# A listed order of operations, seven chunk maxima instead of eight, and the 1e-9 moved off VectorE, in a fused top-32 attention and tanh-softplus MLP kernel

## The chip, the cores and the metric

The kernel runs on one core of one Trainium2 chip. The metric is device time in microseconds (us): the median of three runs before the change is 825.11 us (824.66 to 825.91). The work is spread over TensorE (PE), VectorE (DVE), ScalarE (ACT), GpSimd (POOL) and the DMA queue that SyncE (SP) feeds.

## The reference

What is computed, for 4 batches of 8 heads, 576 positions and a head dimension of 64, then 2304 tokens of width 512 through a hidden width of 2048:

```python
scores = scale * np.matmul(q, k.transpose(0, 1, 3, 2))
kth = np.partition(scores, -32, axis=-1)[..., -32:-31]
scores = np.where(scores >= kth, scores, -1e9)
scores = scores - np.max(scores, axis=-1, keepdims=True)
attn = np.exp(scores)
attn = attn / (np.sum(attn, axis=-1, keepdims=True) + 1e-09)
x = np.matmul(attn, v)                      # then heads side by side: 2304 x 512
h = x @ w_in                                # 512 -> 2048
sp = np.where(h > 20.0, h, np.log1p(np.exp(np.minimum(h, 20.0))))
out = (h * np.tanh(sp)) @ w_out             # 2048 -> 512
```

## The kernel before

**Attention.** Work comes in 80 units; a unit is one pair of heads and 128 query rows of each (two row tiles, 64 units) or the last 64 rows of both heads (one row tile, 16 units): 144 row tiles in all. For each row tile, PE multiplies queries by keys in two halves of 288 columns (L593), and ACT copies each half out of PSUM into the tile S (L612). DVE takes the eight largest values of each of eight chunks of 72 columns with MAX8 (L627), and from these 64 candidates three times the eight largest (L637, with a match-and-replace between, L641): the 24th largest candidate. It counts how many scores lie below that (L660 on DVE, or L656 on ACT), POOL clears the larger ones (L664), and one MAX8 over the whole row (L670) gives the true 32nd largest, whatever up to eight large values the candidates had missed. ACT takes the exponent (L734), DVE masks it and sums it (L736), DVE adds 1e-9 to the sum (L742, one instruction per row tile) and takes the reciprocal (L743). In the first 21 units the reciprocal is spread (L751) and multiplied in at the very end; in the units after them (`divided`) the row itself is multiplied by it (L764 on POOL or L766 on ACT). PE transposes the weights (L789), ACT copies them (L795); the last pieces are transposed apart (L804 to L808, called the tail here), ACT copies these (L813, tile WX), and PE multiplies with the values (L827, called AV here). The result goes to `xr` (L841 to L848 on DVE, L868 on ACT).

**MLP.** Nine groups of 256 tokens. Each is split into a high and a low part (L923 to L934), so that fp32 products come from three fast matmuls: layer 1 is 144 sets of 12 matmuls (L957) and layer 2 is 144 sets of six (L1042; four plain ones, L1038, in the first group). ACT makes the activation between them (L963 to L989), POOL multiplies and splits (L1004 to L1019). While the first groups run, the weights are unpacked and split; that of some weight tiles goes through PE (L507, L508).

**Order.** `Plan.schedule()` orders the program before it is built: each operation has a cost, its dependencies, a priority and sometimes several engines (`also`); the planner takes the operation that can begin first, by its costs, and the order in which they come out is the order of each engine's queue. The numbers at the head of the file (`OFF`, `LAG`, `CB`, `LB`, ...) are its priorities and choices. PE, DVE, ACT and POOL each run their queue in order, so an instruction that waits holds everything behind it. Where PE would idle in the plan, throw-away matmuls (`filler`, L1162) are put in. A second program follows for inputs in which a row's candidates missed more than eight values; it is branched over (`missed`).

Of the kernel before, what the change touches and what calls it, by code (L numbers as in the profile page):

```python
# [2 lines left out]

# [10 lines left out]
AF = mybir.ActivationFunctionType  # L14
ALU = mybir.AluOpType
# [7 lines left out]

THREE = 2.0 ** -29 * (1 - 2.0 ** -14)
HALF = 0.5 - 2.0 ** -12
NCH = 8
PAD = 9

DIVIDED = 21
HUGE = 1.0e38  # L30
GT = 256
NU = 2
# [6 lines left out]
MLP0 = 76.30575001803295  # L39
MLPS = 1.2378480913699303  # L40
LAG = (-40.12243341145539, -38.28909365751999, -32.8778952976761, -78.28015271904145, -52.599446352806034, -50.1764095795117, -49.69230946190221, -93.44342581700634, 42.99260706506286)
OFF = (-170.39780068367187, -64.02958231418937, -74.2557654138884, 7.857637984216179, -16.336484036288216, -27.809736477494315, -70.41929461728364, -109.81289668550335, -354.7823787851044, -3.8461291151298846, -8.182769269493052, 3.2344209413047413, 6.677364896275946)
WPO = 10.505571910776663
CB = (0, 1, 2, 3, 4, 5, 6, 7, 9, 12, 13, 14, 15, 16, 17, 18, 19, 20, 21, 22, 23, 24, 25, 27, 30, 32, 33, 34, 35, 36, 39, 41, 42, 43, 44, 46, 47, 49, 53, 55, 65, 78, 103, 105, 108, 120, 128, 137)
MB = (0, 4, 5, 10, 14, 16, 21, 31, 34, 35, 42, 45, 74, 134, 135, 143)
PBO = (0, 2, 6, 8, 10, 12)
PBH = (0, 6, 9, 10, 16, 20, 28, 31)
WPR = (13.170210396787844, 0.40696336778296444)
DELTA = {'pe': 0.1566540244821026, 'dve': 0.05973313251400048, 'act': 0.16389989721877987, 'pool': 0.0006081253308147598, 'sp': 0.0}
LOADW = 0.6048073411328094  # L50
ALSO = True
PLAIN = ()
LOST = (0, 1, 2, 3, 4, 5, 6, 8, 9, 10, 12, 13, 14)
LATER = 1
NST = 3
X = (-40.29362652876879, -6.877857684025652)
LOCK = True
BEHIND = 6.0
GATE = 0.17
TAB = 1.295  # L60
BIAS = [(61.900462734716776, 1.2804919633935512), (566.4514881009378, 0.8850565354570911), (1000000000.0, 0.3893476774127522)]
LB = (0, 1, 3, 5, 6, 7, 8, 10, 12, 13, 14, 16, 19, 20, 25, 30)
SB = (6, 10, 15, 17, 25, 30)
PH = {}

SLACK = {'pe': 0.0, 'dve': 0.005961469571805072, 'act': 0.07441473974429097, 'pool': 0.048459337826946364}

CHAIN = 46.48753167278615  # L70
# [33 lines left out]
class Plan:  # L104
# [29 lines left out]
    def schedule(self):  # L134
        free = {p: [(0.0, i) for i in range(n)] for p, n in self.sizes.items()}
# [14 lines left out]
        ndone = 0  # L150
# [3 lines left out]
        loaded, window, left = "exp", None, 0  # L154
# [14 lines left out]

        while ndone < len(self.ops):  # L170
            best = {}
            for c in cand:
                o, rs = c
                if o.tab and window and (o.tab == "exp" or o.tab[1] != window):
                    continue
                pr = pool_ready(o) if o.alloc else 0.0
                if pr is None:
                    continue
                w = None
                for x, (e, d, _) in enumerate(o.ways):  # L180
# [23 lines left out]
            o = c[0]  # L204
# [97 lines left out]
def attn_moe_kernel(  # L302
# [17 lines left out]
    T = S // 128  # L320
    L = S - T * 128
    HS = S // 2
    CW = S // NCH
    NG = NT // GT
    scale = 1.0 / math.sqrt(D)
    Z = SIZES
# [73 lines left out]
    def build(fast, weights):  # L400
# [157 lines left out]
        def unit(b, p, t, pkey, kready, vready, last, pr, final):  # L558
# [59 lines left out]
            if fast:  # L618
# [1 line left out]
                Ct = lambda n: g_("C", ck[n])  # L620
                cur = [None] * nt
                for n in range(nt):
                    per = NCH // 2
                    for e in range(2):
                        def mx(n=n, e=e):
                            for j in range(e * per, (e + 1) * per):
                                nc.vector.max(Ct(n)[:, j, :], St(n)[:, j * CW:(j + 1) * CW])  # L627
                        al = [("C", ck[n])] if e == 0 else []
                        if n == 0 and e == 0:
                            al += [("M8", m8k), ("SM", smk)]  # L630
                        dd = [sready[n][e], cur[n]]
# [598 lines left out]
```

## Time and profile before

| | |
|---|---|
| median of three runs | 825.11 us |
| profiled execution, its own time | 824.54 us |
| its span, first to last instruction | 822.7 us |
| PE busy | 773.6 us (94%) |
| DVE busy | 685.1 us (83%) |
| ACT busy | 631.4 us (77%) |
| POOL busy | 561.0 us (68%) |
| mean granted PE clock | 0.981 of full speed |

Busy is the time in which at least one instruction of an engine was under way; DVE and PE overlap the end of one instruction with the start of the next, so the pace of a row of equal instructions is read from their starts, not from the duration of one. A wait in the profile names the instruction that came late and the one that released it.

### The profile page before, as it was taken

What the parts mean: (1) busy time and instruction counts of PE and PEld (TensorE: products, weight loads), DVE (VectorE), ACT (ScalarE), POOL (GpSimd) and SP (SyncE); (2) the same over time, 40 slices, a digit from 0 to 9 for tenths busy, and PEclk for the clock granted to TensorE, in tenths of its full rate; (3) what the DMA queues carried; (4) which work ended last, traced back from release to release, by engine and by line L of the source; (5) the groups of instructions that cost most, each with busy time, mean ns of one, the idle gap of its engine ahead of it and who ended that gap; (6) DMA issues with size and microseconds to landing.
All of it is one profiled execution on the core that took longest, in us unless ns stands there. A gap on an engine that the chain in (4) does not pass through costs nothing.

```text
span 822.7 us, 18268 instructions
## 1 busy us (share of the span) xinstructions
PE 773.6 (94%) x5698; PEld 604.1 (73%) x5698; DVE 685.1 (83%) x3344; ACT 631.4 (77%) x1245; POOL 561.0 (68%) x821
## 2 busy tenths in 40 slices
PE   7988999988998899999989999999999999999996
PEld 5556578656667687878857777778878787788884
DVE  7999999998898899998999899899999998715031
ACT  6889899898897687978797567887887698556380
POOL 4888786889898887697688775688666565703111
PEclk9999999996999999999999999999999999999998
DMA  4444346782224233231123332222322213403322
GB/s 155 131 127 125 99 145 202 228 284 89 89 95 144 61 93 93 67 110 38 40 64 95 109 101 85 65 82 79 91 82 73 80 59 91 128 21 92 102 75 83
DMA packets 56795, 83.73 MB, mean 102 GB/s; under 512 B 5872, under 2 KB 28656, under 8 KB 56688
## 3 DMA queue, kind: packets, MB, share of 16 engines
q1 hardware_dynamic: 56464, 82.19, 32.7%
q8 instruction: 47, 0.77, 0.4%
q14 instruction: 60, 0.49, 0.2%
q10 hardware_dynamic: 224, 0.28, 0.1%
HBM read 66.72 MB, written 8.13 MB: 91 GB/s over the span
## 4 chain that ended last, share of the span: by engine, by line
PE 65%; DVE 14%; POOL 9%; ACT 7%; issue 3%; DMA 1%; SPq 0%; DVEq 0%; POOLq 0%
PE psH L957 20%; PE psO L1042 18%; PE psW L593 8%; PE psW L827 7%; PE psW L789 6%; POOL Y L664 3%; DVE Y L736 3%; DVE C L627 3%; PE psO L1038 2%; PE psW L957 2%; DVE M L670 2%; DVE Y L660 2%; DVE M L637 1%; DVE C L641 1%; ACT mb L963 1%
## 5 line engine op out<-in xcount | busy, mean ns | idle before, releaser
L664 POOL TENSOR_TENSOR Y<-Y,S 128x576 f32<-128x576 f32 x126 | 177.4, 1419 | 37.7 <-DVE Y L736 13.3
L627 DVE MAX8 C<-S 128x8 f32<-128x72 f32 x1152 | 176.3, 219 | 13.6 <-ACT S L612 13.5
L957 PE MATMUL psH<-xh,wih 128*128 128x256 f32 x528 | 158.8, 301 | 6.3 <-ACT mb L963 5.5
L957 PE MATMUL psH<-xl,wih 128*128 128x256 f32 x528 | 148.1, 280 | 0.6 <-POOL xl L928 0.6
L957 PE MATMUL psH<-xh,wil 128*128 128x256 f32 x528 | 147.8, 280 | 0.0
L1019 POOL TENSOR_TENSOR GL<-mb,GH 128x256 fp32r<-128x256 f32 x102 | 74.7, 736 | 78.0 <-PE psO L1042 61.2
L593 PE MATMUL psW<-KS,QS 64*128 64x288 f32 (+1 forms) x576 | 117.7, 457 | 5.5 <-ACT S L612 2.9
L612 ACT COPY S<-psW 128x288 f32<-128x288 f32 x288 | 100.7, 407 | 22.9 <-PE psW L593 21.5
L670 DVE MAX8 M<-Y 128x8 f32<-128x585 f32 x144 | 109.5, 762 | 9.7 <-POOL Y L664 7.9
L957 PEld LDWEIGHTS psH<-xh,wih 128*128 128x128 f32 x528 | 99.8, 189 | 20.4 <-ACT mb L963 8.5
L734 ACT ACTIVATE Y<-S,SM 128x576 f32<-128x576 f32 x121 | 92.8, 783 | 25.1 <-DVE M L670 24.6
L736 DVE SCALAR_TENSOR_TENSOR Y<-S,M,Y 128x576 f32<-128x576 f32 x121 | 103.2, 876 | 8.2 <-ACT Y L734 7.9
L1042 PE MATMUL psO<-woh,GH 128*128 128x512 f32 x256 | 108.3, 423 | 0.0
L957 PEld LDWEIGHTS psH<-xl,wih 128*128 128x128 f32 x528 | 100.0, 189 | 1.3 <-POOL xl L928 0.8
L957 PEld LDWEIGHTS psH<-xh,wil 128*128 128x128 f32 x528 | 99.8, 189 | 0.0
L789 PE MATMUL psW<-ident,Y 128*128 128x128 f32 (+1 forms) x640 | 85.3, 276 | 12.8 <-POOL Y L764 4.3
L795 ACT COPY WT<-psW 128x512 f32<-128x512 f32 (+1 forms) x159 | 80.9, 547 | 20.1 <-PE psW L789 19.4
L789 PEld LDWEIGHTS psW<-ident,Y 128*128 128x128 f32 (+1 forms) x640 | 66.6, 144 | 37.9 <-POOL Y L764 8.9
L827 PE MATMUL psW<-WT,V 128*64 128x128 f32 (+1 forms) x1280 | 82.3, 272 | 10.6 <-ACT WX L813 10.6
L827 PEld LDWEIGHTS psW<-WT,V 128*64 128x64 f32 x1280 | 64.4, 139 | 32.5 <-ACT WX L813 16.2
L593 PEld LDWEIGHTS psW<-KS,QS 64*128 64x128 f32 (+1 forms) x576 | 58.7, 192 | 37.0 <-issue 12.3
L660 DVE TENSOR_SCALAR_CACHE_REDUCE Y<-S,M 128x576 f32<-128x576 f32 x96 | 77.0, 806 | 7.9 <-PE psW L806 6.1
(155 smaller groups left out, 1748.2 us busy)
## 6 DMA issues: line engine op xcount, KB each, us to landing
WL<-wld SPq DMA_DIRECT2D x104, 256.0 KB, 2.7
V<-in_v_dram SPq DMA_DIRECT2D x28, 320.0 KB, 3.0
mb<-in_moe_w_in_dram SPq DMA_DIRECT2D x16, 512.0 KB, 3.9
mb<-in_moe_w_out_dram SPq DMA_DIRECT2D x16, 512.0 KB, 4.2
KS<-in_k_dram SPq DMA_DIRECT2D x27, 288.0 KB, 2.9
QS<-in_q_dram SPq DMA_DIRECT2D x80, 64.0 KB, 2.1
woh<-mb SPq DMA_DIRECT2D x16, 256.0 KB, 3.3
wld<-woh SPq DMA_DIRECT2D x13, 256.0 KB, 2.4
```

The lines of the kernel that those rows point to most:

```text
L593: nc.tensor.matmul(psW[P.slot[wks[n]]][:, 0:HS], g_("QS", qs)[hp, :], KSt()[hp, rng], start=True, stop=True)
L612: return lambda: eng(St(n)[:, rng], psW[P.slot[w]][:, 0:HS])
L627: nc.vector.max(Ct(n)[:, j, :], St(n)[:, j * CW:(j + 1) * CW])
L660: c = P.op("dve", dve(S, 60), lambda n=n, c24=c24, lt=lt: nc.vector.tensor_scalar(Yt(n), St(n), c24(), None, op0=ALU.is_lt, op1=ALU.add, a ...
L664: y = either(pool2(S), held(S), lambda eng, n=n: eng.tensor_tensor(Yt(n), Yt(n), St(n), op=ALU.mult), [c], prio=pr + 0.5 + OFF[5])
L670: ym.append(P.op("dve", dve(S + PAD), lambda n=n: nc.vector.max(M8()[:, n, 3, :], Yw(n)), [y, x], prio=pr + 0.6 + OFF[6]))
L734: e = P.op("act", acts(S, 1), lambda n=n: nc.scalar.activation(Yt(n), St(n), AF.Exp, scale=scale, bias=SM()[:, 0, n:n + 1]), [nm, ym[n]], ...
L736: mk.append(P.op("dve", held(S, 68), lambda n=n: nc.vector.scalar_tensor_tensor(Yt(n), St(n), th(n), Yt(n), op0=ALU.is_ge, op1=ALU.mult, a ...
L789: nc.tensor.transpose(psW[P.slot[wk]][:, t_ * w:(t_ + 1) * w], Yt(n)[hp, c_:c_ + 128], ident[hp, hp])
L827: nc.tensor.matmul(psX[64 * h:64 * h + 64, 0:n_], lw, rhs, start=t_ == 0, stop=t_ == T)
L957: nc.tensor.matmul(w, a, b_, start=n == 0, stop=n == len(mm) - 1)
L1042: nc.tensor.matmul(psO[t], c[:, ts_], y, start=f == 0 and n == 0, stop=f == NF - 1 and n == 2)
```

## The change

Four things. (1) `CHUNKS` replaces the eight chunks of 72 columns by seven of 83 or 82; three of them lie in the first half of S, four end in the second. The tiles of candidates have 56 values, not 64. (2) The two instructions per unit that add 1e-9 leave DVE; one instruction on POOL or ACT adds it for the whole unit, and the reciprocal on DVE waits for that. (3) `DIVIDED` goes from 21 to 20, and the planner's numbers are others. (4) The first program's order is no longer what the planner picks: `listed()` unpacks a string of numbers, one operation and one choice of engine each, and `schedule()` takes the operations in that order (it still works out when each would start, and the queues follow these starts).

```diff
-NCH = 8
+CHUNKS = (83, 83, 82, 82, 82, 82, 82)
-DIVIDED = 21
+DIVIDED = 20
-LB = (0, 1, 3, 5, 6, 7, 8, 10, 12, 13, 14, 16, 19, 20, 25, 30)
+LB = (0, 1, 3, 5, 7, 8, 10, 13, 14, 20, 22, 24, 27, 29, 31)
...
+ORDER = (
+    b"c-m!G2OyR2_rLCS-97ES_uiF^>^&pNXoyG}8cIb)*`rCzC|X7(gp8<2Q8Fq*i!_KdQ1XAC_r2)*`=5L7^PKZJpYu8AdEQGIc>DU@kR_29W6gZ?"
...
+def listed():
+    x = np.frombuffer(zlib.decompress(base64.b85decode(ORDER)), np.uint8).reshape(2, -1).astype(int)
+    x = x[0] + 256 * x[1]
+    return [(int(n) & 8191, int(n) >> 13) for n in x]
...
         while ndone < len(self.ops):
             best = {}
+            want, only = self.listed[ndone] if self.listed else (None, None)
             for c in cand:
                 o, rs = c
-                if o.tab and window and (o.tab == "exp" or o.tab[1] != window):
+                if self.listed:
+                    if o.seq != want:
+                        continue
+                elif o.tab and window and (o.tab == "exp" or o.tab[1] != window):
                     continue
...
                 for x, (e, d, _) in enumerate(o.ways):
+                    if only is not None and x != only:
+                        continue
...
-                        def mx(n=n, e=e):
-                            for j in range(e * per, (e + 1) * per):
-                                nc.vector.max(Ct(n)[:, j, :], St(n)[:, j * CW:(j + 1) * CW])
+                        js = [j for j in range(NCH) if (EDGE[j + 1] > HS) == e]
+
+                        def mx(n=n, js=js):
+                            for j in js:
+                                nc.vector.max(Ct(n)[:, j, :], St(n)[:, EDGE[j]:EDGE[j + 1]])
...
             def rz():
-                for n in range(nt):
-                    nc.vector.tensor_scalar(SM()[:, 3, n:n + 1], SM()[:, 2, n:n + 1], 1e-9, None, op0=ALU.add)
                 nc.vector.reciprocal(SM()[:, 4, 0:nt], SM()[:, 3, 0:nt])

-            rzo = P.op("dve", 0.25, rz, mk + [lg], free=[("M8", m8k)], prio=pr + 0.8 + OFF[6])
+            rzo = P.op("pool", 0.15, lambda: nc.gpsimd.tensor_scalar(
+                SM()[:, 3, 0:nt], SM()[:, 2, 0:nt], 1e-9, 0.0, op0=ALU.add, op1=ALU.add), mk, prio=pr + 0.8 + OFF[6],
+                also=[("act", acts(nt), lambda: nc.scalar.activation(
+                    SM()[:, 3, 0:nt], SM()[:, 2, 0:nt], AF.Copy, bias=1e-9))] if ALSO else ())
+            rzo = P.op("dve", 0.13, rz, [rzo, lg], free=[("M8", m8k)], prio=pr + 0.8 + OFF[6])
```

Two places show what that does to the queues. The first is DVE's queue at the reciprocal of the 26th unit (SM is the tile of that unit's sums, Y its weights, C the candidates, M8 the maxima). Before:

```order
L736 SCALAR_TENSOR_TENSOR Y_1_92,SM_1_106<-S_4_89,M8_1_103,Y_1_92 128x576
L736 SCALAR_TENSOR_TENSOR Y_1_92,SM_1_106<-S_5_90,M8_1_103,Y_1_92 128x576
L627 MAX C_1_117<-S_3_88 128x8 x4
L742 TENSOR_SCALAR SM_1_106<-SM_1_106 128x1 x2
L743 RECIPROCAL SM_1_106<-SM_1_106 128x2
L797 COPY WT_1_100<-psW3_127 128x512
```

The same unit in the changed kernel:

```order
L845 SCALAR_TENSOR_TENSOR Y_1_92,SM_1_106<-S_4_89,M8_1_103,Y_1_92 128x576
L875 TENSOR_SCALAR Y_0_91<-Y_0_91,SM_0_105 128x576
L845 SCALAR_TENSOR_TENSOR Y_1_92,SM_1_106<-S_5_90,M8_1_103,Y_1_92 128x576
L736 MAX C_0_116<-S_3_88 128x8 x7
L850 RECIPROCAL SM_1_106<-SM_1_106 128x2
L746 MAX M8_0_102<-C_0_116 128x8
```

The two additions are gone from this queue, seven chunk maxima stand between the last sum and the reciprocal, and one multiplication of an earlier unit's row (L875) has come over from POOL.

The second is PE's queue at the tail and the AV of the 59th unit (psW is the PSUM bank of the attention, WT and V its weights and values, psO that of layer 2). Before:

```order
L593 MATMUL psW_124<-KS_93,QS_97 128x288
L593 MATMUL psW_126<-KS_93,QS_97 128x288
L806 MATMUL psW_125<-ident,Y_91 128x128
L827 MATMUL psW_125<-WT_99,V_98 64x128
L827 MATMUL psW_125<-WT_100,V_98 64x128
```

The same unit in the changed kernel:

```order
L917 MATMUL psW_125<-ident,Y_91 128x128
L1153 MATMUL psO<-woh,GH_110 128x512
L1153 MATMUL psO<-WL_82,GH_110 128x512
L1153 MATMUL psO<-woh,GL_113 128x512
L1153 MATMUL psO<-woh,GH_110 128x512
L1153 MATMUL psO<-WL_82,GH_110 128x512
L1153 MATMUL psO<-woh,GL_113 128x512
L701 MATMUL psW_127<-KS_93,QS_97 128x288
L701 MATMUL psW_126<-KS_93,QS_97 128x288
L938 MATMUL psW_125<-WT_99,V_98 64x128
L938 MATMUL psW_125<-WT_100,V_98 64x128
```

Between the tail (L806, now L917) and the AV (L827, now L938) of one unit there stood nothing; now a set of layer 2 and a pair of scores stand there.

## Rows read from the trace of the kernel before

**Rows 1.** Busy time by stage, with the granted PE clock (1.00 is full)

```profile
core 0: us, PE busy (x) PEld busy (x) DVE busy (x) ACT busy (x) POOL busy (x), PEclk, DMA share, GB/s
0.00:107.20 107.20, 93.33 (x597) 61.65 (x597) 97.34 (x522) 88.96 (x203) 80.05 (x144) 0.98 0.42 126
107.20:538.20 431.00, 408.47 (x3137) 315.45 (x3133) 396.69 (x1997) 348.80 (x696) 339.29 (x469) 0.97 0.35 109
538.20:721.80 183.60, 181.25 (x1383) 146.90 (x1382) 167.36 (x778) 145.07 (x277) 124.69 (x184) 1.00 0.28 85
721.80:815.20 93.40, 90.47 (x589) 80.06 (x588) 23.71 (x51) 47.63 (x68) 17.01 (x26) 1.00 0.26 76
815.20:822.70 7.50, 0.04 (x1) 0.00 (x0) 0.00 (x0) 0.92 (x3) 0.00 (x0) 0.69 0.28 76
```

**Rows 2.** What PE waited for: total us, times, longest

```profile
PE psW L827 <- ACT WX L813: 10.6, 16, 1.6
PE psH L957 <- ACT mb L963: 5.5, 11, 1.0
```

**Rows 3.** Busy time from 184 to 200 us, columns as in rows 1

```profile
184.00:200.00 16.00, 13.86 (x84) 10.54 (x83) 14.52 (x73) 13.83 (x27) 14.15 (x22) 0.50 0.30 107
```

**Rows 4.** DVE in order of time: start, us, line, operation, count

```profile
480.40 0.20 DVE L742 TENSOR_SCALAR SM<-SM 128x1 f32<-128x1 f32 x2
480.64 0.17 DVE L743 RECIPROCAL SM<-SM 128x2 f32<-128x2 f32 x1
...
484.02 1.18 DVE L627 MAX8 C<-S 128x8 f32<-128x72 f32 x8
485.11 0.80 DVE L736 SCALAR_TENSOR_TENSOR Y<-S,M,Y 128x576 f32<-128x576 f32 x1
```

**Rows 5.** Groups by line: count, busy us, mean ns, idle before

```profile
L627 DVE MAX8 C<-S 128x8 f32<-128x72 f32 x1152 | 176.3, 219 | 13.6 <-ACT S L612 13.5
L670 DVE MAX8 M<-Y 128x8 f32<-128x585 f32 x144 | 109.5, 762 | 9.7 <-POOL Y L664 7.9 <-POOL Y L667 0.9
L637 DVE MAX8 M<-C 128x8 f32<-128x64 f32 x432 | 80.7, 215 | 0.8
L641 DVE MATCH_REPLACE8 C<-M,C 128x64 f32<-128x64 f32 x288 | 59.0, 209 | 0.0
L766 ACT ACTIVATE Y<-Y,SM 128x576 f32<-128x576 f32 x39 | 30.2, 780 | 11.1 <-DVE SM L743 11.1
L643 POOL TENSOR_SCALAR SM<-M 128x2 f32<-128x2 f32 (+1 forms) x80 | 15.9, 198 | 13.2 <-DVE Y L736 5.5 <-DVE Y L664 3.7 <-DVE SM L742 2.8
L988 ACT ACTIVATE scr<-half 128x1 f32<-128x1 f32 x18 | 3.7, 203 | 0.2
```

**Rows 6.** PE in order of time, at two weight pieces, columns as in rows 4

```profile
94.00 1.17 PE L507 MATMUL psW<-mb,ident 128*128 128x512 f32 x2
94.58 0.82 PE L508 MATMUL psW<-wih,minus 128*128 128x512 f32 x1
95.33 0.76 PE L593 MATMUL psW<-KS,QS 64*128 64x288 f32 x4
```

**Rows 7.** PE in order of time, at a pair of scores, and at four

```profile
403.71 0.76 PE L593 MATMUL psW<-KS,QS 64*128 64x288 f32 x4
404.39 0.66 PE L789 MATMUL psW<-ident,Y 128*128 128x128 f32 x4
...
530.10 1.24 PE L593 MATMUL psW<-KS,QS 64*128 64x288 f32 x8
531.27 0.50 PE L1042 MATMUL psO<-woh,GH 128*128 128x512 f32 x1
```

**Rows 8.** PE in order of time, from a tail to its AV

```profile
406.31 0.27 PE L806 MATMUL psW<-ident,Y 128*128 128x128 f32 x1
...
407.71 0.28 PE L957 MATMUL psH<-xh,wil 128*128 128x256 f32 x1
408.83 1.09 PE L827 MATMUL psW<-WT,V 128*64 128x128 f32 x16 [0.84 <-ACT WX L813]
```

More of the change, by code (lines that the diff above doesn't have):

```diff
@@ L1 @@
+import base64
 from contextlib import ExitStack
 import math
+import zlib
+import numpy as np
 import concourse.bass as bass
@@ L38 @@
 XR = 512
[L39 to L50, printed above, removed]
+MLP0 = 99.9471825342185
+MLPS = 1.3046593286706494
+LAG = (-61.945234399878714, -28.560387665490126, -30.733466152330276, -49.99226948223787, -39.59170297278783, -37.763623947039065, -32.50062373683786, -31.73557493089706, 69.0203084459386)
+OFF = (-270.837867949834, -126.52133585008643, -75.32111061042728, 24.19914748288818, -59.87508736281464, -62.150670896667066, -73.07028630855159, -142.397960199234, -386.09854039881225, 8.435102366991714, -0.3272910054271826, 9.914407474972224, -0.8667673702698865)
+WPO = -3.242106378627835
+CB = (0, 1, 2, 3, 4, 5, 6, 7, 9, 12, 13, 14, 15, 16, 17, 18, 19, 20, 21, 22, 23, 24, 25, 27, 30, 32, 33, 34, 35, 36, 39, 41, 42, 43, 44, 46, 47, 49, 53, 54, 78, 105, 108, 120, 128, 137)
+MB = (0, 4, 5, 12, 14, 16, 20, 21, 26, 31, 34, 35, 42, 45, 74, 134, 135, 143)
+PBO = (2, 8, 12, 16)
+PBH = (0, 2, 6, 10, 20, 28, 31, 138)
+WPR = (-58.942102111632416, 3.1617121716635608)
+DELTA = {'pe': 0.16045153795699024, 'dve': 0.05837958824185292, 'act': 0.16483333678555037, 'pool': 0.0, 'sp': 0.0}
+LOADW = 0.5973225490946582
 ALSO = True
@@ L55 @@
 NST = 3
-X = (-40.29362652876879, -6.877857684025652)
+X = (59.27722256788873, -6.849812527005892)
 LOCK = True
@@ L60 @@
 TAB = 1.295
-BIAS = [(61.900462734716776, 1.2804919633935512), (566.4514881009378, 0.8850565354570911), (1000000000.0, 0.3893476774127522)]
-LB = (0, 1, 3, 5, 6, 7, 8, 10, 12, 13, 14, 16, 19, 20, 25, 30)
-SB = (6, 10, 15, 17, 25, 30)
+BIAS = [(61.38914879277713, 1.2862143784541045), (555.744362882396, 0.8844329061263839), (1000000000.0, 0.13497106279125548)]
+LB = (0, 1, 3, 5, 7, 8, 10, 13, 14, 20, 22, 24, 27, 29, 31)
+SB = (6, 8, 15, 17, 25, 30)
 PH = {}
-SLACK = {'pe': 0.0, 'dve': 0.005961469571805072, 'act': 0.07441473974429097, 'pool': 0.048459337826946364}
-CHAIN = 46.48753167278615
+SLACK = {'pe': 0.00041215485209543704, 'dve': 0.005889892243299891, 'act': 0.06381358280261656, 'pool': 0.046882349621389305}
+CHAIN = 204.2899463159386
 FILL = (0.5, 0.7)
@@ L116, in __init__ @@
         self.filler = None
+        self.listed = None
     TURN = {("full", "full"): 0.0, ("full", "turn"): 0.09, ("full", "rows"): 0.14, ("full", "cols"): 0.18,
@@ L322, in attn_moe_kernel @@
     HS = S // 2
-    CW = S // NCH
+    NCH = len(CHUNKS)
+    EDGE = [sum(CHUNKS[:j]) for j in range(NCH + 1)]
+    assert EDGE[-1] == S
     NG = NT // GT
@@ L622, in unit @@
                 for n in range(nt):
-                    per = NCH // 2
                     for e in range(2):
-                        def mx(n=n, e=e):
-                            for j in range(e * per, (e + 1) * per):
-                                nc.vector.max(Ct(n)[:, j, :], St(n)[:, j * CW:(j + 1) * CW])
+                        js = [j for j in range(NCH) if (EDGE[j + 1] > HS) == e]
+                        def mx(n=n, js=js):
+                            for j in js:
+                                nc.vector.max(Ct(n)[:, j, :], St(n)[:, EDGE[j]:EDGE[j + 1]])
                         al = [("C", ck[n])] if e == 0 else []
@@ L633, in unit @@
                             dd.append(cur[0])
-                        cur[n] = P.op("dve", per * 0.1367, mx, dd, alloc=al, prio=pr + 0.1 + OFF[3])
+                        cur[n] = P.op("dve", sum(1.0417 * CHUNKS[j] + 62 for j in js) / 1000, mx, dd, alloc=al, prio=pr + 0.1 + OFF[3])
                 for r in range(3):
                     for n in range(nt):
-                        cur[n] = P.op("dve", dve(64), lambda n=n, r=r: nc.vector.max(M8()[:, n, r, :], Ct(n)),
+                        cur[n] = P.op("dve", dve(8 * NCH), lambda n=n, r=r: nc.vector.max(M8()[:, n, r, :], Ct(n)),
                                       [cur[n]], free=[("C", ck[n])] if r == 2 else (), prio=pr + 0.2 + OFF[3])
@@ L640, in unit @@
                         for n in range(nt):
-                            cur[n] = P.op("dve", 0.19, lambda n=n, r=r: nc.vector.match_replace(
+                            cur[n] = P.op("dve", dve(8 * NCH, 52), lambda n=n, r=r: nc.vector.match_replace(
                                 Ct(n), M8()[:, n, r, :], Ct(n), NEG), [cur[n]], prio=pr + 0.2 + OFF[3])
@@ L1159, in program @@
         if fast:
+            P.listed = listed()
+            assert len(P.listed) == len(P.ops)
+        if fast:
             def filler(m):
```

83 lines of the change are left out of this document (added).

## The prediction

> **What bounds the kernel now.** I read the stage table first, then the waits of PE, then single stretches of PE and DVE. In the stage table [rows 1] the reader is to see two engines that are both nearly full, in turn. From 538 us on PE is the bound: 181.3 of 183.6 us, then 90.5 of 93.4 us. Before that PE idles 107.2 - 93.3 = 13.9 us in the first stage, where no MLP work exists yet, and 431.0 - 408.5 = 22.5 us in the long middle. DVE works 91% of the first stage and 92% of the middle. So DVE's attention sets when MLP work becomes ready, and PE falls idle when neither is at hand. Behind PE's last matmul lie 7.5 us of eviction and output.
>
> The waits of PE [rows 2] show where the idle time goes: 10.6 us in 16 waits are for ACT's copy of the tail, right ahead of an AV. One of them [rows 8]: the tail starts at 406.31, the last layer-1 matmul put behind it at 407.71, the AV only at 408.83, after 0.84 us of waiting. The cover was one MLP set, and it was too short by that much. [...]
>
> **The change part by part.**
>
> *DVE.* Eight chunk maxima start within 485.11 - 484.02 = 1.09 us [rows 4], so 0.136 us each. From 72 to 585 values a MAX8 grows from 219 to 762 ns [rows 5], 1.06 ns per value; one over 82.3 values then takes 0.147 us, seven take 1.03. That is 0.06 us per row tile, times 144: 8.6 us. The passes over the candidates shrink by 8 values: 432 maxima and 288 replacements [rows 5] at 8 x 1.06 = 8.5 ns: 6.1 us. The additions of 1e-9 took 480.64 - 480.40 = 0.24 us for a unit of two tiles [rows 4]; 64 such units and 16 of about 0.18 make 18.2 us. Together DVE's own row work falls by 33 us. In return the listed order sends other work to DVE: by counts in the order 17 more copies of transposed weights, 10 more low parts of x, 10 more of layer 2's splits, 15 more of other evictions; it takes 47 copies to `xr` away. Priced by their nearest kin, DVE's queue up to its last reciprocal is shorter by about 17 us, and almost all of that is in its second half: 3 to 4 us up to the 40th reciprocal, 15 by the 59th.
>
> *ACT.* It takes over 33 row multiplications of 0.78 us [rows 5] = 25.7, 42 additions of 1e-9 (a 128x1 ACTIVATE takes 203 ns [rows 5]) = 8.5, 48 copies to `xr`, 17 spreads of the reciprocal and 14 high parts of x, some 23 us together by copies of like size, and gives up 17 copies of transposed weights and some evictions, about 12: 45 us more. In the middle stage ACT goes from 81% busy [rows 1] to about 87%. POOL loses 36 row multiplications and some 40 other pieces and gains 38 additions of 0.198 us (the like-sized instruction at L643 [rows 5]); it gets lighter by some 50 us.
>
> [...]
>
> *The hop.* The reciprocal now waits for POOL or ACT, where DVE did the addition 0.24 us ahead of it. In the changed queue other work of a median 1.1 us stands between a unit's last sum and its reciprocal, as the 26th unit shows (seven maxima, 1.0 us). The addition takes about 0.2 us with a short crossing on either side, so DVE itself is covered. It costs at least nothing, and at most one POOL multiplication (L664, near 1.4 us) on units that have little slack; I take nothing, and keep 3 us for the upper end.
>
> *PE.* Two weight pieces fewer go through PE: 95.33 - 94.00 = 1.33 us each [rows 6], 2.7 us less. One more divided unit saves one transpose, and three more throw-away matmuls cost about as much again: nothing. The AVs get more cover. Counting PE's queue with the paces of the trace, the cover that falls short of 1 us sums to 9.9 us in the order before, which is about what the trace shows (10.6 [rows 2]), and to 5.7 in the listed order; sets with only one MLP set between tail and AV, as in rows 8, fall from 69 of 80 to about 34, the others mostly getting a pair of scores besides, as at the 59th unit. I take 6 us off; at least 4, at most all 10.6. This has a price: scores stand in 139 runs, not 108. A pair takes 404.39 - 403.71 = 0.68 us, four together 531.27 - 530.10 = 1.17 [rows 7], so a split costs 0.19: 31 x 0.19 = 5.9 us. Some of it comes back where an AV now follows scores rather than an MLP set; I take 5, between 0 and 5.9.
>
> *The stages.* In the first one group 0 of the MLP starts behind 8 AVs of the order, not 10: PE has 11 us less work ahead of it, so that layer 1 fills time in which PE idled or ran fillers. Of the 13.9 us idle I take 4 off (none to 10). In the middle DVE's queue shrinks by about 11 us between the 20th and the 59th reciprocal; PE's other idle time there (22.5 less its share of AV waits, some 15) falls by 4.5 (none to 12). The half-clock stretch may shrink or move: 3 off, between 8 gained and 8 lost. After 538 us PE is full, and only its own terms count. The output's end stays 7.5 us.
>
> *Sum.* -2.7 + 5 - 6 - 4 - 4.5 - 3 = -15.2 us, less 2 for what ACT's heavier queue gives back: -13. From the profiled execution's 824.5 that is 811.3; the median of the runs shown is 0.6 above that execution, which is within their spread, so I say **811.5 us**.
>
> **The rivals.**
>
> *ACT becomes the one that PE waits for (slower).* For it speaks that PE's largest waits already end on ACT [rows 2], and that ACT takes 45 us more. Its free share in the middle stage falls from 19% to 13%. If waits on it grew as that share shrinks, the 16 us of rows 2 would become 24, the copies that free `psW` (S, WT) would come late by as much again, none of the gains in the stages would come, and the splits would cost 5.9: 824.5 + 8 + 8 + 5.9 - 2.7 = 844 at worst, about 830 if half of it. It decides as soon as PE's waits on ACT copies grow by over 13 us in sum. Against it: the cover ahead of the AVs grew, and the copies are short.
>
> *PE was the bound all along (the same).* PE keeps its 773 us of work, the splits eat what the waits give back, and idle time only changes its place: 824 to 826 us. For it speaks the 94%; against it that 36 us of idle time lie before 538 us with DVE at 92% there.
>
> *DVE sets the pace to the end (much faster).* Then all 17 us of its shorter queue come off the last reciprocal, at 92% busy 18 us, and since 13 us less PE work are left behind the last AV in the listed order, the end would come up to 31 us earlier: 794 us. Against it: PE would have to lose two thirds of its idle time, and it is full from 538 us on.
>
> *The clock.* [...] As a mechanism here: one more stretch like that of rows 3, at another place of the new order, costs 8 us on top of the 3 not gained, and the time is 822; losing the old one without a new one gives 806. Both lie within the range.
>
> *The change does not do what it says.* Seven chunks could miss more than eight values of a row and run the second program, which would about double the time. On the reference's inputs the worst row misses 6 or fewer: no chance given.
>
> **How the numbers follow.** Main case, 800 to 820 us: 0.62; DVE's pace to the end, under 800: 0.09; one more half-clock stretch, 820 to 823.5: 0.08; the same: 0.07; ACT, or a wait of the new order that I do not see, slower: 0.14. A measurement of this kernel can tell 0.2% from no change, 1.65 us. So faster 0.79, same 0.07, slower 0.14. The range of 8 in 10 reaches from 799 to 825: it leaves about 0.07 below and 0.13 above; the costs bounded above (3 us of hops, 8 of the clock, 10 of the first stage) lie in it.
>
> **What would show it.** In the profile after: DVE's busy time lower by some 12 us, ACT's higher by about 45, POOL's lower by about 50; PE's waits for the tail's copy at 4 to 6 us; the first layer-1 matmul some 10 to 15 us before 107; PE's idle time up to the start of group 5 down from 36 us to about 25; scores on PE dearer by about 5 us. The prediction is wrong if PE's waits on ACT grow, if DVE idles ahead of its reciprocals, or if the PE clock falls to half for longer than before.

## The result, and the profile after

The median went from 824.88 us (823.54 to 825.91) to **804.62 us** (803.22 to 807.12), a ratio of 0.9759 with a 95% interval of [0.9730, 0.9787]. The direction was forecast and the time lies in the range, but the move is 20 us where 13 were forecast.

The profiled execution took 804.39 us, its span 802.5. The view by stretches, cut at the changed kernel's own bounds (first layer-1 matmul, start of group 5, last reciprocal, last matmul), answers to [rows 1]; the columns are the same.

```profile
core 0: us, PE busy (x) PEld busy (x) DVE busy (x) ACT busy (x) POOL busy (x), PEclk, DMA share, GB/s
0.00:94.20 94.20, 79.81 (x510) 52.48 (x511) 83.00 (x418) 80.83 (x191) 70.18 (x122) 0.98 0.43 130
94.20:520.20 426.00, 412.47 (x3244) 320.21 (x3243) 402.03 (x1876) 381.68 (x821) 316.21 (x456) 1.00 0.36 114
520.20:711.90 191.70, 188.57 (x1434) 154.31 (x1434) 165.24 (x713) 150.06 (x297) 112.84 (x165) 1.00 0.26 79
711.90:793.60 81.70, 80.73 (x516) 70.35 (x514) 28.99 (x63) 45.07 (x63) 19.55 (x24) 1.00 0.31 87
793.60:802.50 8.90, 0.00 (x1) 0.00 (x0) 0.00 (x0) 0.92 (x3) 0.00 (x0) 0.69 0.29 71
```

Three things are to be seen. DVE is no less full in the middle (402 of 426 us, 94%, against 92%), so it was not given room. PE's idle time up to group 5 fell from 36.4 us to 14.4 + 13.5 = 27.9. And the granted clock of the middle is 1.00, not 0.97.

Where the 20.2 us of span came from can be read off the starts of the MLP groups on PE (first layer-1 matmul of each, us):

| | g0 | g1 | g2 | g3 | g4 | g5 | g6 | g7 | g8 | last matmul ends |
|---|---|---|---|---|---|---|---|---|---|---|
| before | 107.2 | 193.0 | 280.4 | 371.2 | 440.4 | 538.2 | 618.7 | 719.3 | 752.9 | 815.2 |
| after | 94.2 | 188.5 | 265.9 | 362.6 | 423.3 | 520.3 | 598.1 | 693.2 | 729.1 | 793.6 |
| gained | 13.0 | 4.5 | 14.5 | 8.6 | 17.1 | 17.9 | 20.6 | 26.1 | 23.8 | 21.6 |

Group 0 starts 13 us sooner, but only 4.5 of that are left at group 1. 13.4 us are won between groups 1 and 5, another 3.7 up to the last matmul, and the output's end gives 1.4 back (8.9 us, not 7.5). A group's start also depends on where the list puts the group, so a single step of the last row (14.5, then 8.6) is not the gain of one stretch.

Up to the start of group 1, PE does not idle less than before. Before and after:

```profile
0.00:193.00 193.00, 173.60 (x1200) 120.46 (x1200) 178.89 (x896) 165.00 (x361) 150.54 (x254) 0.97 0.52 164
```

```profile
0.00:188.50 188.50, 167.28 (x1197) 115.65 (x1197) 172.52 (x819) 170.32 (x393) 148.86 (x243) 0.98 0.49 154
```

Its idle time there is 193.0 - 173.6 = 19.4 us before and 188.5 - 167.3 = 21.2 after; the 4.5 us come out of its busy time.

By another cut of the same 20.2 us, PE's busy time fell by 12.0, its idle time before the last matmul by 9.7. Of the 12.0, the clock can account for about 10, an estimate: over stretches of 10 us each, up to the last matmuls, the time at the lower level, 0.50, sums to 27.2 us before and 6.8 after, and half the difference is 10.2. (By the pace of layer 1's matmuls before, which start 0.21 us apart from 193.3 us on, at 0.50, and 0.12 us apart from 644.2 us on, at 1.00, it is 9.2.) This splits busy time; it does not show that the clock is what the end waited for (see e7 below). The stretch of [rows 3] now reads

```profile
184.00:200.00 16.00, 13.99 (x91) 9.63 (x92) 15.65 (x68) 15.41 (x29) 13.56 (x18) 0.89 0.49 161
```

with the clock at 0.89, not 0.50. At full clock, by the same estimate, PE has almost the same work in both kernels: 773.6 - 13.6 = 760.0 and 761.6 - 3.4 = 758.2 us.

What PE waited for (total, times, longest) answers to [rows 2]:

```profile
PE psW L938 <- ACT WX L924: 6.3, 8, 1.5
PE psH L1068 <- ACT mb L1074: 3.1, 5, 1.1
PE psW L900 <- ACT Y L877: 3.0, 5, 1.1
```

The wait of an AV for the tail's copy fell from 10.6 to 6.3 us. One that is left shows why the rest stays; this is PE in order of time, as in [rows 8]:

```profile
353.00 0.27 PE L917 MATMUL psW<-ident,Y 128*128 128x128 f32 x1
353.97 1.09 PE L938 MATMUL psW<-WT,V 128*64 128x128 f32 x16 [0.70 <-ACT WX L924]
```

Here nothing at all stands between tail and AV. The list has such places too.

The groups by line answer to [rows 5] and carry the moved work:

```profile
L736 DVE MAX8 C<-S 128x8 f32<-128x82 f32 (+1 forms) x1008 | 170.8, 230 | 8.7 <-ACT S L720 7.9 <-ACT WT L906 0.3
L746 DVE MAX8 M<-C 128x8 f32<-128x56 f32 x432 | 83.4, 208 | 1.8
L750 DVE MATCH_REPLACE8 C<-M,C 128x56 f32<-128x56 f32 x288 | 57.3, 200 | 0.0
L877 ACT ACTIVATE Y<-Y,SM 128x576 f32<-128x576 f32 x72 | 56.1, 786 | 3.0 <-DVE SM L850 2.7
L850 DVE RECIPROCAL SM<-SM 128x2 f32<-128x2 f32 (+1 forms) x80 | 12.3, 153 | 9.6 <-POOL SM L852 7.2 <-ACT SM L854 2.1
L852 POOL TENSOR_SCALAR SM<-SM 128x2 f32<-128x2 f32 (+1 forms) x38 | 9.0, 237 | 29.2 <-DVE Y L845 16.3 <-ACT Y L839 9.6 <-DVE GL L1130 1.4
L854 ACT ACTIVATE SM<-SM 128x2 f32<-128x2 f32 (+1 forms) x42 | 8.9, 213 | 9.2 <-DVE Y L845 9.1
```

Over the whole span DVE's busy time fell by 5.8 us to 679.3, ACT's rose by 27.2 to 658.6, POOL's fell by 42.2 to 518.8.

Last, the largest waits between 200 and 600 us on any engine but SP, of the kernel before and then of the one after:

```profile
ACT Y L734 <- DVE M L670: 20.2, 20, 2.7
ACT WT L795 <- PE psW L789: 13.6, 19, 2.8
ACT mb L963 <- PE psH L957: 13.5, 18, 1.7
```

```profile
POOL klog L782 <- DVE Y L845: 24.5, 13, 3.0
POOL SM L852 <- DVE Y L845: 14.3, 7, 4.3
ACT S L720 <- PE psW L701: 9.6, 18, 1.5
```

Before, ACT waited longest, for DVE's maxima (L734 is the exp) and for PE's transposes. After, the longest waits lie on POOL, the engine with the most free time, and that of the exp (L843) stands further down:

```profile
ACT Y L843 <- DVE M L779: 5.3, 10, 1.3
```

### The profile page after: what moved, and what is told of

Read it like the earlier page. It is cut to its first block, busy times and chain, and to the rows that moved or that the text cites. A ratio compares the mean times of both kernels' runs of the same rounds, so it can differ in the third digit from the quotient of the medians.

```text
span 802.5 us, 17921 instructions
## 1 busy us (share of the span) xinstructions
PE 761.6 (95%) x5697; PEld 597.3 (74%) x5697; DVE 679.3 (85%) x3067; ACT 658.6 (82%) x1372; POOL 518.8 (65%) x765
## 4 chain that ended last, share of the span: by engine, by line
PE 61%; ACT 14%; DVE 9%; POOL 7%; issue 3%; DMA 3%; SPq 0%; ACTq 0%; POOLq 0%; DVEq 0%
PE psO L1153 19%; PE psH L1068 19%; PE psW L701 7%; PE psW L938 7%; PE psW L900 5%; POOL Y L773 3%; DVE Y L845 2%; ACT S L720 2%; ACT tb L1100 2%; DVE C L736 1%; ACT Y L843 1%; PE psW L1068 1%; DVE M L779 1%; PE psO L1149 1%; ACT WT L906 1%
## 5 line engine op out<-in xcount | busy, mean ns | idle before, releaser
L773 POOL TENSOR_TENSOR Y<-Y,S 128x576 f32<-128x576 f32 x126 | 178.4, 1422 | 27.4 <-DVE Y L845 8.2
L736 DVE MAX8 C<-S 128x8 f32<-128x82 f32 (+1 forms) x1008 | 170.8, 230 | 8.7 <-ACT S L720 7.9
L1068 PE MATMUL psH<-xh,wih 128*128 128x256 f32 x544 | 163.1, 300 | 4.8 <-ACT mb L1074 3.1
L1068 PE MATMUL psH<-xl,wih 128*128 128x256 f32 x544 | 153.6, 282 | 0.0
L1068 PE MATMUL psH<-xh,wil 128*128 128x256 f32 x544 | 153.4, 282 | 0.0
L701 PE MATMUL psW<-KS,QS 64*128 64x288 f32 (+1 forms) x576 | 121.1, 459 | 4.6 <-DMA QS<-in_q_dram 2.1
L720 ACT COPY S<-psW 128x288 f32<-128x288 f32 x288 | 108.9, 406 | 18.5 <-PE psW L701 18.0
L1068 PEld LDWEIGHTS psH<-xh,wih 128*128 128x128 f32 x544 | 103.7, 191 | 15.5 <-ACT mb L1074 5.8
L845 DVE SCALAR_TENSOR_TENSOR Y<-S,M,Y 128x576 f32<-128x576 f32 x120 | 99.4, 841 | 7.2 <-ACT Y L843 6.8
L843 ACT ACTIVATE Y<-S,SM 128x576 f32<-128x576 f32 x120 | 93.4, 785 | 11.6 <-DVE M L779 10.9
L1130 POOL TENSOR_TENSOR GL<-mb,GH 128x256 fp32r<-128x256 f32 x93 | 69.4, 750 | 46.2 <-DVE GH L1120 22.5
L900 PE MATMUL psW<-ident,Y 128*128 128x128 f32 (+1 forms) x640 | 82.3, 270 | 10.9 <-ACT Y L877 3.0
L938 PEld LDWEIGHTS psW<-WT,V 128*64 128x64 f32 x1280 | 64.2, 138 | 33.6 <-ACT WX L924 14.8
L938 PE MATMUL psW<-WT,V 128*64 128x128 f32 (+1 forms) x1280 | 81.9, 271 | 6.8 <-ACT WX L924 6.3
L906 ACT COPY WT<-psW 128x512 f32<-128x512 f32 (+1 forms) x142 | 74.5, 553 | 15.5 <-PE psW L900 15.2
L746 DVE MAX8 M<-C 128x8 f32<-128x56 f32 x432 | 83.4, 208 | 1.8
```

Source lines behind the costliest of these rows:

```text
L701: nc.tensor.matmul(psW[P.slot[wks[n]]][:, 0:HS], g_("QS", qs)[hp, :], KSt()[hp, rng], start=True, stop=True)
L720: return lambda: eng(St(n)[:, rng], psW[P.slot[w]][:, 0:HS])
L736: nc.vector.max(Ct(n)[:, j, :], St(n)[:, EDGE[j]:EDGE[j + 1]])
L746: cur[n] = P.op("dve", dve(8 * NCH), lambda n=n, r=r: nc.vector.max(M8()[:, n, r, :], Ct(n)), [cur[n]], free=[("C", ck[n])] if r == 2 else ...
L773: y = either(pool2(S), held(S), lambda eng, n=n: eng.tensor_tensor(Yt(n), Yt(n), St(n), op=ALU.mult), [c], prio=pr + 0.5 + OFF[5])
L843: e = P.op("act", acts(S, 1), lambda n=n: nc.scalar.activation(Yt(n), St(n), AF.Exp, scale=scale, bias=SM()[:, 0, n:n + 1]), [nm, ym[n]], ...
```

## The experiments

The theory at the start was that the order and DVE's relief work together: DVE at 92% of the middle sets when MLP work is ready. The rivals were the order alone, the relief alone, POOL's relief, PE as the bound, the half-clock stretch, and the cover of the AVs. "Order held" means that the operations, their engines, their buffers and the throw-away matmuls stay word for word those of the kernel named, by means of a list like the change's own.

**The new order without the reliefs.** `e1_new_order_eight` is the changed kernel with eight chunks, order held.

```diff
-CHUNKS = (83, 83, 82, 82, 82, 82, 82)
+CHUNKS = (72,) * 8
```

> The changed kernel with eight chunks of 72 columns again; the listed order, the engines and the banks stay word for word. DVE gets back 8.6 us of chunk maxima and 6.1 us of passes over 64 instead of 56 candidates. Theory 'order and relief together' (mine): with DVE over 92% busy up to the last reciprocal about half of that shows, 810 to 814 us. Rival 'the order alone': within 2 us of the changed kernel's 804.6. Rival 'DVE sets the pace': all of it shows, 819.

Measured: 805.85 us, 0.9770 [0.9745, 0.9795].

`e2_new_order_adds_dve` puts the 1e-9 back on DVE, directly ahead of the reciprocal, and empties the operation on POOL or ACT.

```diff
+                for n in range(nt):
+                    nc.vector.tensor_scalar(SM()[:, 3, n:n + 1], SM()[:, 2, n:n + 1], 1e-9, None, op0=ALU.add)
                 nc.vector.reciprocal(SM()[:, 4, 0:nt], SM()[:, 3, 0:nt])
```

> The changed kernel with the 1e-9 added by DVE again, right ahead of each reciprocal; POOL and ACT no longer do it, all else stays in its listed place. DVE gets back 18.2 us of additions and loses the 9.3 us in which its reciprocals waited for POOL or ACT; ACT and POOL lose 8.9 and 9.0 us. Theory 'together': 807 to 811 us. Rival 'the order alone': 803 to 806. Rival 'DVE sets the pace': 18.2 - 9.3 = 9 us more, 813.

Measured: 803.25 us, 0.9737 [0.9710, 0.9764].

`e4_new_order_no_add` has no addition anywhere. It leaves out only that: a row's sum is at least 1, so 1e-9 vanishes in fp32.

```diff
-                nc.vector.reciprocal(SM()[:, 4, 0:nt], SM()[:, 3, 0:nt])
+                nc.vector.reciprocal(SM()[:, 4, 0:nt], SM()[:, 2, 0:nt])
```

> The changed kernel without the addition of 1e-9 at all: the reciprocal reads the sum itself, which is at least 1 since each row's largest exponent is 1, so that 1e-9 vanishes in fp32; this part of the computation is left out. Listed order otherwise the same. DVE's 9.3 us of waits for the addition go, ACT and POOL get 9 us lighter each. Theory 'together': 800 to 803 us. Rival 'the order alone', in which these waits are hidden: 804 to 805. Rival 'DVE sets the pace': 795.

Measured: 801.83 us, 0.9723 [0.9698, 0.9748], the lowest median of all. Its interval overlaps that of the changed kernel, so it is surely better than the kernel before, and not shown to be better than the change. All five of its executions (800.52 to 803.09) lie below the four of the changed kernel (803.22 to 807.12), so the addition and its hop may still cost up to about 3 us.

The busy times of the page, of e1 and of e2:

```profile
PE 759.3 (94%) x5697; PEld 595.5 (74%) x5697; DVE 689.5 (86%) x3211; ACT 659.6 (82%) x1372; POOL 517.3 (64%) x765
```

```profile
PE 763.4 (95%) x5697; PEld 598.6 (74%) x5697; DVE 688.1 (86%) x3211; ACT 653.6 (81%) x1330; POOL 505.4 (63%) x727
```

In both, DVE is busier than in the kernel before (685.1 us), and the time is still about 20 us shorter. Neither part of the relief is needed for the gain, taken back one at a time; the new order with both taken back was not run. The hop to POOL or ACT costs nothing that e2 can tell.

**The reliefs without the new order.** `e5_old_order_seven_no_add`: order of before held, seven chunks, and no addition of 1e-9.

```diff
-NCH = 8
+CHUNKS = (83, 83, 82, 82, 82, 82, 82)
-                for n in range(nt):
-                    nc.vector.tensor_scalar(SM()[:, 3, n:n + 1], SM()[:, 2, n:n + 1], 1e-9, None, op0=ALU.add)
-                nc.vector.reciprocal(SM()[:, 4, 0:nt], SM()[:, 3, 0:nt])
+                nc.vector.reciprocal(SM()[:, 4, 0:nt], SM()[:, 2, 0:nt])
```

> The kernel before, its own order held fixed by a list, with seven chunks and without the addition of 1e-9 (left out here; the sums are at least 1, so nothing changes in fp32). DVE loses 8.6 + 6.1 + 18.2 = 33 us of its 685 and nothing else changes its place. Theory 'together': 812 to 819 us, since PE's idle time ahead of 538 us shrinks but the half-clock stretch and the thin cover ahead of the AVs stay. Rival 'the order alone': 822 to 825. Rival 'DVE sets the pace': 792 to 798.

Measured: 825.65 us, 1.0012 [0.9995, 1.0029]. The busy times of its page, the stretch from 107.2 to 538.2 us, and the wait of the exp between 200 and 600 us:

```profile
PE 778.0 (94%) x5698; PEld 609.2 (74%) x5698; DVE 663.6 (80%) x3056; ACT 631.7 (76%) x1245; POOL 564.3 (68%) x821
```

```profile
107.20:538.20 431.00, 410.12 (x3108) 317.99 (x3108) 381.83 (x1810) 345.98 (x689) 339.17 (x465) 0.96 0.36 109
```

```profile
ACT Y L836 <- DVE M L772: 18.5, 16, 2.7
```

Against [rows 1] DVE has 14.9 us less work in this stretch and PE does about as much in it. All of DVE's relief (21.5 us of its busy time over the span) turned into waiting, and the exp waits for DVE's maxima almost as long as before (20.2 us). With e1 and e2 this is the reverse of the theory: the list, that is its order with its choices of engines, brings the gain with either relief taken back, and both reliefs without the list bring none.

**Less work for PE, in either order.** `e11_old_order_less_pe` and `e12_new_order_less_pe` leave out one of layer 2's products (n == 1) in groups 1 to 5, so the output isn't the reference's. That is 160 matmuls at a pitch of 0.23 us (their starts in the kernel before, from 640.92 to 641.84 us), an estimated 37 us. The order of before is held in e11, that of the change in e12.

```diff
+                            if fast and 1 <= g <= 5 and n == 1:
+                                continue
```

> The kernel before, its order held fixed, with the middle product (high part by low weights) left out of layer 2 in groups 1 to 5: 160 matmul pairs, 80 sets times 2 times 0.232 us = 37 us less work on PE between 200 and 620 us; that part of the sum is missing from the output. Theory 'PE is full there and sets the time': 790 to 802 us. Rival 'the attention's chain through the other queues sets it': 815 to 825, PE only idles more.

> The changed kernel with the same 37 us of layer 2's middle product left out in groups 1 to 5 (that part of the sum is missing from the output). Theory 'PE is full there and sets the time': 768 to 780 us. Rival 'the attention's chain sets it': 795 to 804.

Measured: e11 824.21 us, 0.9991 [0.9974, 1.0007]; e12 792.91 us, 0.9612 [0.9577, 0.9646], 11.7 below the changed kernel. In the order of before, 37 us less work for the busiest engine is worth nothing; in the new one it is worth a third. The busy times of e11's page, and the same stretch:

```profile
PE 752.0 (91%) x5538; PEld 579.2 (70%) x5538; DVE 683.8 (83%) x3344; ACT 629.9 (77%) x1245; POOL 561.4 (68%) x821
```

```profile
107.20:538.20 431.00, 397.44 (x3038) 301.71 (x3038) 395.79 (x1996) 348.03 (x698) 339.42 (x469) 0.96 0.35 109
```

PE idles 33.6 us in it, not 22.5, and DVE's work is as before. Over the span PE's busy time fell by 21.6 us, all of which turned into waiting. That it did not fall by 37 is in part the clock's doing, by the estimate made above: the time at the lower level rose from 27.2 to 41.2 us, which is about 7 us of busy time. The chain that ended last tells who took over. Its shares by engine, of before, of e5 and of e11, in that order:

```profile
PE 65%; DVE 14%; POOL 9%; ACT 7%; issue 3%; DMA 1%; SPq 0%; DVEq 0%; POOLq 0%
```

```profile
PE 74%; ACT 8%; DVE 7%; POOL 7%; issue 2%; DMA 1%; SPq 0%; ACTq 0%; POOLq 0%; DVEq 0%
```

```profile
PE 45%; DVE 28%; POOL 11%; ACT 10%; issue 4%; DMA 0%; SPq 0%; DVEq 0%; POOLq 0%; ACTq 0%
```

Relieve DVE, and its part of the chain halves while PE's grows; relieve PE, and DVE's part doubles. The length stays: in a fixed order the path seems to hand itself to the neighbour. These are shares of one execution each; e7 below, in which neither was relieved, has 71% for PE and 11% for DVE, so e5's step is small beside e11's. Relief of ACT, and of two engines at once, was not tried.

In the order of before, the busy shares (94% for PE, 83% for DVE) do not tell which of the two sets the end: DVE (e5) was relieved, PE (e11) too, and neither moved it. In the new order PE's relief did (e12).

**POOL's relief.** The change takes 36 row multiplications from POOL. `e6_old_order_pool_to_act` moves 34 of POOL's 67 to ACT, order of before held; `e9_new_order_act_to_pool` moves 36 of ACT's 72 back to POOL in the changed kernel.

```diff
+            if fast and o.seq in TO_ACT:
+                o.eng, _, o.fn = o.ways[2]
```

> The kernel before, its order held fixed, with every second of POOL's 67 row multiplications given to ACT at the same place of the order (34; the listed order moves 36 away from POOL). Theory 'POOL was late at the starved points' (at 266 and 425 us the chain of waits before runs through five POOL instructions in a row): PE's idle time from 240 to 280 and 400 to 440 us, 4.9 and 4.7, falls by half and two half-clock spells go, 815 to 820 us. Rival 'places, not engines': 823 to 826. Rival 'ACT is full': slower than 828.

```diff
+            if fast and o.seq in TO_POOL:
+                o.eng, _, o.fn = o.ways[0]
```

> The changed kernel with every second of ACT's 72 row multiplications back on POOL (36, the number that left it), at the same place of the order. Theory 'POOL was late': 810 to 816 us. Rival 'places, not engines': 803 to 806.

Measured: e6 826.88 us, 1.0023 [1.0009, 1.0037]; e9 813.41 us, 0.9863 [0.9849, 0.9877]. So POOL's relief, at ACT's cost, is worth nothing alone, and taking as much of it back (every second multiplication, not the ones that had moved) costs 9 us in the new order. PE's largest wait in e9:

```profile
PE psW L903 <- POOL Y L878: 7.0, 14, 1.1
```

Transposes now wait for POOL's products, which in the changed kernel they hardly did (1.7 us in 3 waits). The choice of engine is a part of the list and can't be exchanged apart from the places around it.

**The half-clock stretch.** `e7_old_order_filled_gaps`: order of before held, 21 throw-away matmuls in the six waits of PE between 180 and 192 us.

```diff
+EXTRA = {1231: 3, 1233: 5, 1235: 4, 1264: 4, 1485: 2, 1268: 3}
+                for _ in range(EXTRA.get(o.seq, 0)):
+                    nc.tensor.matmul(psHH[:, 0:128], ident, ident, start=True, stop=True)
```

> The kernel before, its order held fixed, with 21 throw-away matmuls on PE in the six waits between 180 and 192 us, where psH is free. Theory 'the clock': PE stays at full clock from 184 to 200 us and the 8 us lost there come back, 816 to 819 us. Rival 'the work there is late anyway' (the engines that feed PE set the time of that stretch): half-clock time goes but 823 to 826 us stay.

Measured: 825.09 us, 1.0011 [0.9995, 1.0026]. Four stretches of e7, then three of them of the kernel before (for the fourth see [rows 3]), then two of e5, in which nothing is filled:

```profile
180.00:184.00 4.00, 3.96 (x34) 3.49 (x35) 3.85 (x23) 4.00 (x10) 3.44 (x10) 1.00 0.61 199
184.00:200.00 16.00, 12.02 (x103) 8.92 (x100) 14.50 (x73) 13.71 (x27) 14.15 (x22) 0.91 0.30 102
270.00:280.00 10.00, 8.41 (x44) 5.34 (x45) 6.51 (x32) 4.65 (x11) 7.82 (x11) 0.66 0.16 51
430.00:440.00 10.00, 9.22 (x40) 6.83 (x41) 8.59 (x57) 7.01 (x13) 9.45 (x11) 0.53 0.08 21
```

```profile
180.00:184.00 4.00, 1.32 (x8) 0.85 (x10) 3.86 (x24) 4.00 (x10) 3.45 (x10) 0.90 0.72 260
270.00:280.00 10.00, 9.22 (x70) 6.56 (x70) 8.35 (x39) 6.83 (x16) 9.17 (x12) 0.90 0.19 50
430.00:440.00 10.00, 10.00 (x76) 7.87 (x77) 8.82 (x41) 9.04 (x12) 10.00 (x14) 1.00 0.35 113
```

```profile
184.00:200.00 16.00, 14.09 (x86) 10.77 (x83) 13.47 (x65) 13.41 (x27) 14.69 (x22) 0.50 0.27 92
430.00:440.00 10.00, 9.76 (x50) 7.69 (x51) 6.70 (x34) 6.48 (x11) 7.72 (x13) 0.71 0.22 63
```

The fill worked where it was put: from 180 to 184 us PE is busy for 3.96 us, not 1.32, and the stretch of [rows 3] behind it is back at 0.91. In this execution two later stretches are lower instead, and the time at the lower level sums to 27.4 us, as before. But that the fill moved the low clock there is not shown. The stretch at 430 us is low in e5 too (in an execution of 827.94 us, a long one as well), with the gap ahead of 184 us unfilled. And the profiled execution of e7 took 829.72 us at a mean clock of 0.982, one of the longest of twelve; eight of the others took 822.98 to 825.52 us at 0.984 to 0.991, where the twenty of the kernel before beside them have 0.977 to 0.987. So in most of them the clock was higher (median 0.987, against 0.98), and the median time stayed where it was.

The clock does not set the time by itself, then: the executions of e7 say so, and e6, whose profiled execution has 17.0 us at the lower level, 10 fewer than before, and took 826.07 us. Within the kernel before the two go together (822.65 to 824.52 us at a mean clock of 0.987, 825.70 to 830.24 at 0.977); which of them brings the other no run shows. What an order of before without any half-clock stretch would take is open.

**The place of the AVs.** `e8_old_order_av_later` puts 66 AVs behind PE's next operation, in the order of before; `e13_new_order_av_earlier` puts 35 AVs one PE operation earlier, in the new order.

```diff
+        order.insert(j, order.pop(i))
```

> The kernel before, its order held fixed, with 66 AVs each put behind the next operation of PE, as the listed order mostly has it. Theory 'cover': PE's 10.6 us of waits for the tail's copy fall to 2 to 4, 817 to 821 us. Rival 'PE idles elsewhere instead': 823 to 826, the same idle time at other waits.

```diff
+        order.insert(between[-1], order.pop(at[s]))
```

> The changed kernel with 35 AVs, those with two or more operations of PE between tail and AV, each moved ahead of the last of these, as the order before mostly has it. Theory 'cover' of the prediction: waits for the tail's copy back to about 10 us, 807 to 811 us. Rival 'the AV's place frees the attention's buffers' (the run with the AVs put later was 37 us slower): 798 to 804. Rival 'places hardly matter': 803 to 806.

Measured: e8 862.08 us, 1.0461 [1.0443, 1.0478]; e13 822.41 us, 0.9960 [0.9937, 0.9983]. First PE's waits for the tail's copy, of e8 and of e13:

```profile
PE psW L953 <- ACT WX L939: 2.3, 4, 1.3
```

```profile
PE psW L959 <- ACT WX L945: 7.0, 10, 1.5
```

In e8 these fell from 10.6 to 2.3 us, just as the theory 'cover' has it, and the kernel is 37 us slower all the same; in e13 they hardly grew (6.3 in the changed kernel). So the wait that the prediction priced explains neither result. The two largest waits of e8 from 200 to 600 us, and the second largest of e13:

```profile
DVE xr L967 <- PE psW L953: 32.4, 25, 3.5
ACT Y L860 <- DVE M L796: 31.4, 27, 4.0
```

```profile
ACT S L741 <- PE psW L722: 23.7, 23, 2.8
```

In e8 the AVs come later by one operation, and DVE stands 32.4 us at the copies of their results; ACT's exp waits 31.4 us for maxima that stand in the same queue. In e13 the AVs go ahead of the scores, and ACT's copy of these waits 23.7 us, not 9.6. The waits are only a part of it. PE's own busy time grew as well, though it has the same matmuls: in e8 from 773.6 to 789.7 us, in e13 from 761.6 to 772.6. The rows of the scores, after and in e13, have much of the latter:

```profile
L701 PE MATMUL psW<-KS,QS 64*128 64x288 f32 (+1 forms) x576 | 121.1, 459 | 4.6 <-DMA QS<-in_q_dram 2.1
```

```profile
L722 PE MATMUL psW<-KS,QS 64*128 64x288 f32 (+1 forms) x576 | 127.8, 458 | 5.9 <-DMA QS<-in_q_dram 2.3
```

The time at the lower clock is 6.8 us in both of these, so it isn't the clock; what lengthens PE's work there is open. One step of one kind of operation, either way, costs 18 to 37 us, more than all of PE's waits for the tail's copy together (10.6 us [rows 2]).

**The new numbers without the list.** `e10_new_numbers_no_list` is the changed kernel with the planner choosing.

```diff
-            P.listed = listed()
+            pass
```

> The changed kernel with its new numbers and both edits, but without the list: the planner picks the order itself. Theory 'the listed order': 815 to 826 us, since the numbers alone do not fill the starved places. Rival 'the numbers': 803 to 808, the list only writes down what the planner does with them.

Measured: 836.02 us, 1.0132 [1.0086, 1.0178]. The planner's numbers alone make the kernel slower, though both reliefs are in it; the 31 us from there to the changed kernel are the list's.

## Why the prediction was right, and where it was not

- **Right: the sign and the range.** Also right: group 0 starts 13 us earlier (10 to 15 forecast); the AVs wait 6.3 us (4 to 6 forecast); PE's idle time up to group 5 is 27.9 us (about 25 forecast); 33 more row multiplications on ACT, at 786 ns.
- **Near by luck: the first stage, -4 us.** It was to come out of PE's idle time. That did not shrink, neither ahead of group 0 (14.4 us, 13.9 before) nor up to group 1 (21.2, 19.4 before). The 4.5 us kept at group 1 are busy time, 6.3 us less of it, for which the prediction has the two weight pieces (2.7) and the clock.
- **Wrong: "DVE's attention sets when MLP work becomes ready".** This step gave the 4.5 us of the middle to DVE's shorter queue. e5 takes 21.5 us of busy time from DVE and gains nothing; e1 leaves DVE at 689.5 us and gains as much as the change, within the noise. What shrank in the middle is not DVE's work but the waits in the chain from scores to AV, ACT's above all: its exp waited 20.2 us for DVE's maxima in the stretch shown, and 5.3 after; 18.5 in e5, and 6.5 in e1, so this goes with the order and not with DVE's load. It is a sign, not the cause: over the whole span of e13 the exp waits 8.3 us, less than the 10.9 of the changed kernel, and e13 is 18 us slower.
- **Wrong as a term: the AVs' cover, -6 us.** The wait itself fell by 4.3. But e8 and e13 show that this does not come off the end by itself: e8 takes 8.3 us out of it and is 37 us slower. An AV's place ties PE's queue to DVE's and ACT's, and moving it costs 18 to 37 us.
- **Mis-sized: the half-clock term, 3 us off, bounded by 8.** The time at the lower level fell from 27.2 to 6.8 us, about 10 us of PE's busy time. Only the stretch of [rows 3] had been counted, which is 16 of the 27. No run shows the 3 or the 8: they are the author's estimates, the 8 being half of the 16 us that [rows 3] has at 0.50. What the runs show in their place is e7: the stretch at 0.91, the median 825.09 us. How much of the 10 us came off the end is not shown; e7, most executions of which had a higher clock than those of the kernel before, won nothing.
- **Mis-sized, without weight: the loads.** The two reliefs took 21.5 us of busy time from DVE (e5), not 33. ACT rose by 27 us, not 45; DVE fell by 5.8, not 12; POOL by 42, not 50. The scores cost PE 121.1 - 117.7 = 3.4 us more, not 5. Per instruction the maxima over 56 candidates became 7 ns shorter and the replacements 9, against the 8.5 forecast, but the busy time of these maxima rose from 80.7 to 83.4 us.
- **A sign of being wrong that came, and meant little: DVE idles ahead of its reciprocals.** It does so for 9.6 us, 9.3 of them for the addition on POOL or ACT. The hop was priced at nothing, with 3 us for the upper end; e2 finds nothing and e4 leaves room for about 3.
- **Not foreseen: 1.4 us more behind the last matmul**, and another 3.7 won between group 5 and the last matmul, where PE was taken for full.
- **The rivals.** ACT got heavier and yet PE's waits on its copies fell, so the slower one didn't come. The clock's good branch, the old half-clock stretch lost without a new one, was put at 806 us, nearest of all to the 804.6 measured; that it is the reason is not shown. "PE was the bound all along" falls by e11 for the order before. In the new order it is nearer: e12 gets 11.7 us of 37.

So the sum came near, with a middle that was too small (13.4 us won between groups 1 and 5) and a reason for it that the runs refute. Part of that is luck: the terms of idle time were too large (6 + 4 + 4.5 = 14.5 us, where 9.7 came) and that of the clock too small. Which of the list's places carries the gain is open. Each of the two pieces of the list that were exchanged (POOL's share, the AVs) cost 9 to 18 us, up to nearly the whole gain, so the pieces don't add up.

## What to carry to other kernels

Where four in-order queues feed one another through a few buffers, high busy shares on two of them (here 94% and 83%) don't say that either is the bound: take a few per cent of work from each in turn, with the order held, and if nothing moves, try another order before cheaper instructions. Here that was worth 20 us, and the relief of DVE nothing. Such an order is best kept whole, since a piece of it that is exchanged can lose much of the gain. Moving one operation to save one wait is to be measured on the whole kernel: it can save the wait and still lose more. And the stretch at a clock of 0.50 stood here behind a gap in PE's work (1.32 us busy of the 4 us ahead of it); with the gap filled it stood at 0.91, and no time was won.

## What was not expected of the hardware

The clock came back where the gap ahead was filled (e7: 0.50 to 0.91 at 184 to 200 us), and the kernel was no faster for it. And PE's busy time depends on the order even where its matmuls and its time at the lower clock do not: 761.6 us after and 772.6 in e13, both with 5697 matmuls and 6.8 us at the lower level, 6.7 of the 11.0 us at the scores.
